# Channel attention and gated convolution: low halves last in each product, one softmax step on GpSimd, the first k loads on a second queue, native rows dealt anew

## The chip, the cores and the metric

The kernel runs on one core of a Trainium2 chip. The metric is device time in microseconds (us) of one launch, lower is better; the number that is compared is the median of several runs. A core has five engines, each with an instruction stream of its own that it works off strictly in order: TensorE (PE in the profile; its weight loads are listed apart as PEld), VectorE (DVE), ScalarE (ACT), GpSimd (POOL) and SyncE (SP, which here only issues DMAs). They meet through semaphores. TensorE writes only to PSUM, and GpSimd has no access to it.

## The reference

Four batches of q, k and v (6336 rows, 256 channels, fp32). First attention over channels, then a gated causal convolution on its result:

```python
qn = q / (np.linalg.norm(q, axis=1, keepdims=True) + 1e-06)
kn = k / (np.linalg.norm(k, axis=1, keepdims=True) + 1e-06)
s = kn.transpose(0, 2, 1) @ qn / tau          # 256 x 256 per batch
a = softmax(s)                                # over the last axis
x = v @ a
gate_pre[t] = sum over k=0..4 of conv_w[k] * x[t - 4 + k]    # zeros ahead of row 0
gate = 1 / (1 + exp(-gate_pre))
out = (gate * (x @ w_val)) @ w_out
```

## The kernel before, in words

**Split operands.** TensorE is fed fp32r, a format that it takes in one pass but which holds fewer bits than fp32. So most operands are split in two: a high half (ScalarE casts to fp32r) and a low half (what is left: GpSimd subtracts the high half from the value). A product is then the sum of three matmuls: high by high, high by low and low by high. A "native" row is not split: q and k go to TensorE as fp32, one matmul where the split takes three, at another speed; it needs the load alone, neither the cast nor the subtraction.

**Tasks and their names.** For each batch:

- `P`, rows of s: q and k come in 17 groups of up to three 128-row slices (`raw`, 384 KB each for q and k; the first group has one slice and 64 rows that are left over). Line 407 casts (`hi<-raw` on ACT), line 410 subtracts (`hi<-raw,hi` on POOL), line 475 adds both 128-channel halves to `s_ps`. `nw` (lines 376 to 379) says how many slices of a group are native. Line 434 squares q and k, and the squares are summed slice by slice on DVE into `acc_ps` or on POOL into `acc` (line 438).
- `M`, the softmax: norms, root, scaling, exponentials, division (`a`, line 556), the high and low half of `a` (`w`, lines 560 and 563), its transpose times w_val (line 579), and the high and low half of that (lines 583 and 586). So `x @ w_val` is computed as v times (a w_val).

For each of 13 steps of up to 508 rows in a batch (52 in all):

- v comes in (four DMAs), DVE transposes it (645), ACT casts (`v_hi`, 649), POOL subtracts (`v_lo`, 652).
- `X`, line 660: v times a, 12 matmuls of 512 columns into two `x_ps` banks. ACT and DVE make the gate from them: line 684 the first tap, line 687 the other four, line 698 the sigmoid. In the last stretch of the program POOL adds one tap (695).
- `U`, line 660 too: v times a w_val, into `val_ps`; DVE multiplies it with the gate (705), ACT casts (`g_hi`, 711), POOL subtracts (`g_lo`, 714).
- `F`, line 726: times w_out, 24 matmuls of 256 columns in two banks; ACT copies them out (736), SP stores (741).

**What sets the order.** The program is not written in the order in which it runs. Each task is given to `Plan` with its engine, a cost in us, what it depends on and which buffers it takes. `line`, at the end of the kernel, fixes only a due order for TensorE; `deadlines` works back from it when each task must be done, and `run` plays the whole program through with the costs, and always gives an engine the task that is due first among those that can start. The order that comes out is emitted, and each engine keeps it. A changed cost or dependency can therefore move tasks anywhere in the program. Buffers: six of `raw`, three of `hi` and of v's halves, two `x_ps` banks, four other PSUM banks.

**The start.** SP issues q and k of the first groups one by one (lines 390 and 392); ACT loads a function table at once (line 267); TensorE fills the time with matmuls on zeros (lines 457 and 464): seven ahead of the first row, two more after each of the two parts of the first group.

**The end.** The last step has two tiles of 120 rows. Both are multiplied into one bank, `o_ps`; ACT copies the first and stores it from its own queue, DVE copies the second and SP stores it (746 to 748).

## Time and profile before

| | |
|---|---|
| median of three runs | 612.95 us (612.79 to 615.64) |
| the profiled execution | 614.12 us, of which the span 612.3 |
| mean granted TensorE clock in it | 0.996 |
| busy: PE, PEld | 595.1 us (97%), 534.7 us (87%) |
| busy: DVE, ACT, POOL | 522.1 us (85%), 475.8 us (78%), 492.8 us (80%) |
| read from HBM, written | 79.18 MB, 25.95 MB |

PE's busy time is not its work: matmuls overlap, and a matmul of 256 columns is listed with 283 ns where the next one starts 120 ns later. So what TensorE loses is read here from waits (of PE and of PEld, with what ended them) and from when the next matmul starts. PEld's waits are somewhat longer than PE's for one and the same stop, since the listed end of the matmul ahead comes late.

### The profile page before, as it was taken

The page shows a single profiled execution, that of the slowest core. Times are in us where ns is not written, and L with a number is a line of the kernel's source. Part 1 is how long each engine was busy: PE and PEld are TensorE (multiplying, and loading weights), DVE is VectorE, ACT ScalarE, POOL GpSimd, SP SyncE. Part 2 cuts the span into 40 slices and gives each one's busy share as a digit, 9 for nine tenths or more (in the row PEclk, how much of TensorE's full clock was granted, in tenths as well). Part 3 has the DMA queues.
Part 4 walks back from the last instruction along what each step waited for, and adds up shares of the span by engine and source line. Part 5 has one row for each costly group of instructions (what it writes and reads, how often), then busy time and mean ns, then how long its engine had stood idle before and what let it go on. Part 6 is the DMA issues. An engine that isn't in the chain of part 4 may idle for free.

```text
span 612.3 us, 10517 instructions
## 1 busy us (share of the span) xinstructions
PE 595.1 (97%) x3660; PEld 534.7 (87%) x3660; DVE 522.1 (85%) x797; ACT 475.8 (78%) x584; POOL 492.8 (80%) x229
## 2 busy tenths in 40 slices
PE   8999899999999899999999999999999999999996
PEld 7987789999889799898998898898988898888885
DVE  3995999999797999989878899989878879888773
ACT  5787888788889787878689989787857776666763
POOL 2895879999969799999994899999963676676743
PEclk9998999999999999999999999999999999999999
DMA  8999957696775397977659678678646244554222
GB/s 280 389 306 297 258 137 162 161 213 146 203 186 176 93 232 181 189 180 197 166 139 208 193 160 215 141 203 194 137 121 137 68 135 102 124 137 120 69 67 87
DMA packets 154913, 105.84 MB, mean 173 GB/s; under 512 B 111083, under 2 KB 137963, under 8 KB 154859
## 3 DMA queue, kind: packets, MB, share of 16 engines
q1 hardware_dynamic: 154724, 105.04, 67.3%
q8 instruction: 29, 0.48, 0.3%
q14 instruction: 25, 0.20, 0.1%
q10 hardware_dynamic: 135, 0.12, 0.1%
HBM read 79.18 MB, written 25.95 MB: 172 GB/s over the span
## 4 chain that ended last, share of the span: by engine, by line
PE 45%; DVE 9%; ACT 6%; POOL 6%; issue 4%; DMA 1%; SPq 1%; POOLq 0%; DVEq 0%; ACTq 0%
PE o_ps L726 13%; PE x_ps L660 12%; PE val_ps L660 11%; PE s_ps L475 9%; DVE gate L687 6%; POOL v_lo L652 2%; POOL g_lo L714 2%; DMA v_raw<-in_v_dram 1%; DVE gate L705 1%; DVE acc_ps L438 1%; POOL hi L410 1%; POOL gate L695 1%; DVE v_raw L645 1%; ACT gate L698 1%; ACT g_hi L711 1%
## 5 line engine op out<-in xcount | busy, mean ns | idle before, releaser
L687 DVE SCALAR_TENSOR_TENSOR gate<-x_ps,wa,gate 128x508 f32<-128x508 f32 (+1 forms) x401 | 271.8, 719 | 42.0 <-ACT gate L684 21.1
L410 POOL TENSOR_TENSOR hi<-raw,hi 128x1536 fp32r<-128x1536 f32 (+2 forms) x61 | 179.9, 2958 | 6.5 <-ACT hi L407 2.9
L714 POOL TENSOR_TENSOR g_lo<-gate,g_hi 128x1016 fp32r<-128x1016 f32 (+2 forms) x52 | 121.1, 2329 | 47.9 <-ACT g_hi L711 47.1
L652 POOL TENSOR_TENSOR v_lo<-v_raw,v_hi 128x1024 fp32r<-128x1024 f32 (+1 forms) x52 | 124.1, 2387 | 23.1 <-ACT v_hi L649 21.8
L660 PE MATMUL x_ps<-v_hi,w 128*128 128x512 f32 (+2 forms) x416 | 135.3, 385 | 5.5 <-DVE gate L687 3.4
L660 PE MATMUL val_ps<-v_hi,w 128*128 128x508 f32 (+1 forms) x416 | 132.5, 381 | 0.0
L475 PE MATMUL s_ps<-hi 128*128 128x256 f32 (+1 forms) x906 | 121.0, 285 | 1.1 <-POOL hi L410 1.1
L438 DVE TENSOR_TENSOR acc_ps<-acc_ps,sq 128x512 f32<-128x512 f32 (+1 forms) x149 | 103.3, 693 | 17.6 <-ACT sq L434 13.8
L475 PEld LDWEIGHTS s_ps<-hi 128*128 128x128 f32 (+1 forms) x906 | 114.8, 196 | 3.8 <-POOL hi L410 2.2
L726 PE MATMUL o_ps<-wo_hi,g_lo 128*127 128x256 f32 (+1 forms) x400 | 113.2, 283 | 2.4 <-POOL g_lo L714 2.1
L726 PE MATMUL o_ps<-wo_hi,g_hi 128*127 128x256 f32 (+1 forms) x400 | 112.9, 282 | 0.0
L726 PE MATMUL o_ps<-wo_lo,g_hi 128*127 128x256 f32 (+1 forms) x400 | 112.6, 281 | 0.0
L434 ACT ACTIVATE sq<-raw 128x1536 f32<-128x1536 f32 (+2 forms) x68 | 95.6, 1409 | 9.6 <-DMA raw<-in_k_dram 6.7
L660 PEld LDWEIGHTS x_ps<-v_hi,w 128*128 128x128 f32 x416 | 77.4, 188 | 21.3 <-issue 4.6
L660 PEld LDWEIGHTS val_ps<-v_hi,w 128*128 128x128 f32 x416 | 77.1, 188 | 14.9
L711 ACT CAST g_hi<-gate 128x1016 fp32r<-128x1016 f32 (+3 forms) x54 | 52.6, 978 | 36.6 <-DVE gate L705 36.4
L660 PE MATMUL x_ps<-v_lo,w 128*128 128x512 f32 (+2 forms) x208 | 79.8, 384 | 1.0 <-POOL v_lo L652 1.0
L407 ACT CAST hi<-raw 128x1536 fp32r<-128x1536 f32 (+2 forms) x61 | 76.1, 1249 | 4.3 <-DMA raw<-in_k_dram 4.3
L660 PE MATMUL val_ps<-v_lo,w 128*128 128x508 f32 (+1 forms) x208 | 79.0, 380 | 0.0
L726 PEld LDWEIGHTS o_ps<-wo_hi,g_lo 128*127 128x127 f32 (+1 forms) x400 | 75.0, 188 | 3.6 <-POOL g_lo L714 3.6
L736 ACT COPY o_sb<-o_ps 127x512 f32<-127x512 f32 (+1 forms) x99 | 56.8, 585 | 26.3 <-PE o_ps L726 26.1
L726 PEld LDWEIGHTS o_ps<-wo_hi,g_hi 128*127 128x127 f32 (+1 forms) x400 | 74.9, 187 | 1.6
(78 smaller groups left out, 762.6 us busy)
## 6 DMA issues: line engine op xcount, KB each, us to landing
raw<-in_q_dram SPq DMA_DIRECT2D x64, 384.0 KB, 6.0
raw<-in_k_dram SPq DMA_DIRECT2D x64, 384.0 KB, 6.3
v_raw<-in_v_dram SPq DMA_DIRECT2D x192, 128.0 KB, 5.6
out_dram<-o_sb SPq DMA_DIRECT2D x48, 448.0 KB, 3.2
out_dram<-o_sb SPq DMA_DIRECT2D x48, 60.0 KB, 3.0
v_raw<-in_v_dram SPq DMA_DIRECT2D x16, 64.0 KB, 2.4
out_dram<-o_sb SPq DMA_DIRECT2D x3, 240.0 KB, 2.6
raw<-in_q_dram SPq DMA_DIRECT2D x4, 128.0 KB, 2.9
```

The costliest lines, as they stand in the source:

```text
L407: nc.scalar.copy(t["hi"][r, js, :, 0, :], t["raw"][r, js, :, :])
L410: nc.gpsimd.tensor_tensor(t["hi"][r, js, :, 1, :], t["raw"][r, js, :, :], t["hi"][r, js, :, 0, :].bitcast(F32), ALU.subtract)
L434: nc.scalar.activation(t["sq"][0:np_, ja:jb], t["raw"][0:np_, ja:jb], AF.Square)
L438: eng.tensor_tensor(st[key][0:np_], st[key][0:np_], t["sq"][0:np_, j], ALU.add)
L475: nc.tensor.matmul(st["s"][:, h, :], lhs, rhs, start=False, stop=stop and h == NH - 1 and n_ == len(ops) - 1)
L652: nc.gpsimd.tensor_tensor(t["vl"][:, :, 0:g, :], t["v"], t["vh"][:, :, 0:g, :].bitcast(F32), ALU.subtract)
L660: nc.tensor.matmul(dst, weights[b][:, which, ws, ch, hs], vs[:, ch, at + lo:at + hi_], start=n_ == 0, stop=n_ == 3 * NH - 1)
L687: nc.vector.scalar_tensor_tensor(t["gate"][:, h, 0:w], t["x", h][:, k_:k_ + w], cw[:, h, k_:k_ + 1], t["gate"][:, h, 0:w], ALU.mult, ALU.add)
L711: nc.scalar.copy(t["gh"][:, hs, 0:w], t["gate"][:, hs, 0:w])
L714: eng.tensor_tensor(t["gl"][:, hs, 0:w], t["gate"][:, hs, 0:w], t["gh"][:, hs, 0:w].bitcast(F32), ALU.subtract)
L726: nc.tensor.matmul(t["o", p][0:rows, u * C:(u + 1) * C], gs[:, h, j * rows:(j + 1) * rows], ws[:, h, :], start=n_ == 0, stop=n_ == 3 * NH - 1)
L736: nc.scalar.copy(t["o_sb"][0:rows, pair[0]:pair[0] + len(pair), :], t["o", p][0:rows, 0:len(pair) * C].rearrange("p (j c) -> p j c", c=C))
```

## The change

It has five parts, and the planner lays the whole program out again with them.

1. In X and U the matmuls that read v's low half come last within each bank, in F those that read g's low half come last over both tiles of a bank (`HEADS`), and rows of s that are split become two tasks: high by high needs the cast alone, the other two the subtraction too. The planner is told by `lead` how much later than the start of a task such an operand is needed. In the first step of each batch, the low half of the softmax's weights comes last instead.
2. The softmax's `low` (before: line 563, DVE) is a GpSimd instruction, with a cost of 1.25 instead of 0.61.
3. The k loads of the first two groups are issued by ACT, and its table load stands behind them. Three instead of six matmuls on zeros follow the first one, and none follows the first slice.
4. Native rows: in batch 0 all slices of groups 0 to 2 and of the last, and two of each other (before: all of 0 to 4); in batch 1 two slices of groups 0 to 4 (before: three of 0 to 3). That is 47 instead of 49.
5. The last step's two tiles go to two banks (`x_ps`), each copied when its own matmuls are done; the store of the step ahead of it is issued in two parts.

```diff
-SIDE = 5
+SIDE = 3
...
-            nw = GROUP if g < SIDE else 2
+            nw = GROUP if g < SIDE or g == NG - 1 else 2
         else:
-            nw = GROUP if b == 1 and g < LEAD else 0
+            nw = 2 if b == 1 and g <= LEAD else 0
...
+                eng = nc.scalar if b == 0 and g < 2 and s else nc.sync
...
+            if (b, g) == (0, 1):
+                tc.keep_in_program_order(nc.scalar.activation(dummy, ones[:, 0:1], AF.Sqrt))
...
             if b == 0:
-                idle(6)
+                idle(3)
...
-            if (b, g) == (0, 0):
+            if (b, g) == (0, 0) and j == n:
                 idle(2)
...
+        for name, side, halves in (("hi", "C", ((0, 0),)), ("lo", "O", ((0, 1), (1, 0)))):
+            for u, (np_, ja, jb) in enumerate(split):
+                for j in range(ja, jb):
+                    task(("P", b, g, j, name), "PE", 0.24 * len(halves), lambda np_=np_, j=j, halves=halves: mms(np_, j, False, halves),
+                         deps=[(side, b, g, u), ("clear", b)], uses=[hi_i, ("s_ps", b)])
...
         def low():
-            nc.vector.tensor_tensor(weights[b][:, 0, 1], t["a"], weights[b][:, 0, 0].bitcast(F32), ALU.subtract)
+            nc.gpsimd.tensor_tensor(weights[b][:, 0, 1], t["a"], weights[b][:, 0, 0].bitcast(F32), ALU.subtract)
...
-            for ch in range(NH):
-                for ws, vs in ((0, th), (0, tl), (1, th)):
...
+            ops = [(ws, vs, ch) for ws, vs in ((0, th), (0, tl), (1, th))[::1 if new and not which else -1] for ch in range(NH)]
+            ops.sort(key=lambda x: (x[0], x[1] is tl) != (0, False))
...
+            ops = [(gs, ws, h) for gs, ws in ((t["gh"], wo_hi), (t["gh"], wo_lo), (t["gl"], wo_hi)) for h in range(NH)]
+            if HEADS:
+                order = [(u, n_) for n_s in (range(2 * NH), range(2 * NH, 3 * NH)) for u in range(len(pairs[p])) for n_ in n_s]
...
+                 lead={("W", n): first_lo if new else last_lo, ("M", b, "low"): last_lo if new else 0} if h == 0 else {})
...
+                 uses=[g_i, o_ps_i], takes=[o_ps_i], lead={x: (0.47 * len(pairs[p]) if HEADS else 0.47) for x in low_done} if p == 0 else {})
```

What this does to the order on the engines, at three places. First TensorE at the end of batch 0's rows and the start of its softmax (`s_ps<-raw`: native rows, two matmuls for a slice; `s_ps<-hi`: split ones, six for a slice; `ones,acc_all`: the norms). Before:

```order
L475 MATMUL s_ps<-hi 128x256 x6
L475 MATMUL s_ps<-raw 128x256 x4
L475 MATMUL s_ps<-hi 128x256 x6
L502 MATMUL o_ps<-ones,acc_all 128x1 x4
L457 MATMUL s_ps<-zeros 128x512
L475 MATMUL s_ps<-raw 128x256 x4
L534 MATMUL o_ps<-diag,ones 128x128 x2
```

With the change:

```order
L481 MATMUL s_ps<-hi 128x256 x6
L481 MATMUL s_ps<-raw 128x256 x6
L514 MATMUL o_ps<-ones,acc_all 128x1 x4
L463 MATMUL s_ps<-zeros 128x512
L481 MATMUL s_ps<-raw 128x256 x4
L546 MATMUL o_ps<-diag,ones 128x128 x2
```

Three native slices now stand between the last split slice and the norms.

Second, TensorE a little later, where the first X of the program waits for the softmax's weights (`ident,a`: the transposes, `wa,at`: the product with w_val). Before:

```order
L475 MATMUL s_ps<-raw 128x256 x18
L569 MATMUL o_ps<-ident,a 128x128 x4
L660 MATMUL x_ps<-v_hi,w 128x508
L660 MATMUL x_ps<-v_lo,w 128x508
L660 MATMUL x_ps<-v_hi,w 128x508 x2
L660 MATMUL x_ps<-v_lo,w 128x508
L660 MATMUL x_ps<-v_hi,w 128x508
L579 MATMUL o_ps<-wa,at 128x256 x4
```

With the change:

```order
L481 MATMUL s_ps<-raw 128x256 x4
L481 MATMUL s_ps<-hi 128x256 x2
L581 MATMUL o_ps<-ident,a 128x128 x4
L481 MATMUL s_ps<-hi 128x256 x4
L591 MATMUL o_ps<-wa,at 128x256 x4
L674 MATMUL x_ps<-v_hi,w 128x508 x2
L674 MATMUL x_ps<-v_lo,w 128x508 x2
L674 MATMUL x_ps<-v_hi,w 128x508 x4
L674 MATMUL x_ps<-v_lo,w 128x508 x2
L674 MATMUL x_ps<-v_hi,w 128x508 x2
```

The product with w_val and rests of rows stand ahead of X, and within X the third that needs the low half of the weights comes last.

Third, GpSimd at the second softmax. Before:

```order
L714 TENSOR_TENSOR g_lo<-gate,g_hi 128x1016
L652 TENSOR_TENSOR v_lo<-v_raw,v_hi 128x2x256
L714 TENSOR_TENSOR g_lo<-gate,g_hi 128x1016
L410 TENSOR_TENSOR hi<-raw,hi 128x6x256 x3
L652 TENSOR_TENSOR v_lo<-v_raw,v_hi 128x1024
```

With the change:

```order
L727 TENSOR_TENSOR g_lo<-gate,g_hi 128x1016
L666 TENSOR_TENSOR v_lo<-v_raw,v_hi 128x2x256
L416 TENSOR_TENSOR hi<-raw,hi 128x6x256
L575 TENSOR_TENSOR w<-a,w 128x512
L416 TENSOR_TENSOR hi<-raw,hi 128x6x256
L727 TENSOR_TENSOR g_lo<-gate,g_hi 128x1016
L666 TENSOR_TENSOR v_lo<-v_raw,v_hi 128x1024
```

`w<-a,w` is the step that was on VectorE. Over the whole program GpSimd is given 4 of these, 19 instead of 14 subtractions for one slice and 44 instead of 45 for three, and 47 instead of 43 additions of squares; VectorE loses the 4 and 4 additions; TensorE has 94 instead of 98 native matmuls of 128 rows, 918 instead of 906 split ones and 9 instead of 14 on zeros.

More of the change, by code (lines that the diff above doesn't have):

```diff
@@ L51, in deadlines @@
             clock += self.tasks[key]["cost"]
-        after = {key: set() for key in self.tasks}
+        after = {key: {} for key in self.tasks}
         for key, t in self.tasks.items():
             for d in t["deps"]:
-                after[d].add(key)
+                after[d][key] = t["lead"].get(d, 0.0)
         self.users, made = {}, {}
@@ L79, in deadlines @@
             own = self.duration(t)
-            late = min((done[x] for x in after[key]), default=clock) - own - HOP - (FLIGHT if isinstance(t["cost"], tuple) else 0)
+            late = min((done[x] + lead for x, lead in after[key].items()), default=clock) - own - HOP - (FLIGHT if isinstance(t["cost"], tuple) else 0)
             if key[0] in "YR":
                 late = min(late, due["F", key[1], key[2] if key[0] == "Y" else 0] + (4 if key[0] == "Y" else 8))
+            if key[0] == "Q":
+                late -= FLIGHT
             late = min(late, WANTED.get(key, clock))
@@ L173, in run @@
             for x in after[key]:
-                at[x] = max(at[x], end)
+                at[x] = max(at[x], end - T[x]["lead"].get(key, 0.0))
                 missing[x] -= 1
@@ L477, in mms @@
                 idle(2)
         if g == 0:
-            task(("clear", b), "PE", 3.0 if b == 0 else 0.3, clear, uses=[("s_ps", b)], takes=[("s_ps", b)])
+            task(("clear", b), "PE", 1.7 if b == 0 else 0.3, clear, uses=[("s_ps", b)], takes=[("s_ps", b)])
             rows_of[b, g].append(("clear", b))
         for np_, j in rows:
-            u = [x for x, (sn, ja, jb) in enumerate(split) if sn == np_ and ja <= j < jb]
-            task(("P", b, g, j), "PE", (0.72 if u else 0.864) + (0.9 if (b, g) == (0, 0) else 0), lambda np_=np_, j=j: mms(np_, j),
-                 deps=[("O", b, g, u[0]) if u else ("L", b, g), ("clear", b)], uses=[raw_i, ("s_ps", b)] + ([hi_i] if u else []))
@@ L604, in softmax_tasks @@
         task(k_("high"), "ACT", 0.52, high, deps=[k_("divide")])
-        task(k_("low"), "DVE", 0.61, low, deps=[k_("high")])
+        task(k_("low"), "POOL", 1.25, low, deps=[k_("high")])
         task(k_("transpose"), "PE", 0.45, transpose, deps=[k_("divide")], uses=[at_i], takes=[at_i])
@@ L635, in step_tasks @@
         end = n == NS - 1
+        new = i == 0
+        first_lo, last_lo = 0.45 * part, 0.9 * part
         def load():
@@ L737, in out_copy, with store @@
                            t["o", p][0:rows, 0:len(pair) * C].rearrange("p (j c) -> p j c", c=C))
[L739 removed]
+        def store(a, z):
             for r0, r1 in even(rows):
[L741 removed]
+                nc.sync.dma_start(out=dst[r0:r1, a:z, :], in_=t["o_sb"][r0:r1, a:z, :])
         def out_end(u):
@@ L745, in out_end @@
             o_end = raw_p.tile([P, C], F32, name="o_end", tag="raw")
-            copy(o_end[0:rows], t["o", 0][0:rows, u * C:(u + 1) * C])
+            copy(o_end[0:rows], t["o", u][0:rows, 0:C])
             for r0, r1 in even(rows):
@@ L773, in step_tasks @@
             val_i = ("bank", n, "val", h)
-            task(("U", n, h), "PE", 1.38 * part, lambda h=h: value(h), deps=[("W", n), ("M", b, "low_w")], uses=[vs_i, val_i], takes=[val_i])
+            task(("U", n, h), "PE", 1.38 * part, lambda h=h: value(h), deps=[("W", n), ("M", b, "low_w")], uses=[vs_i, val_i], takes=[val_i],
+                 lead={("M", b, "low_w"): last_lo if new and h == 0 else 0})
             task(("B", n, h), "DVE", 0.06 + 0.54 * part, lambda h=h: times(h), deps=[("U", n, h), ("Z", n)], uses=[val_i, gate_i])
```

75 lines of the change are left out of this document (41 added, 34 removed).

## The prediction, made before the changed kernel was run

> **What bounds the kernel now.** I read the shares and the chain of waits first, then the windows, then PE's and PEld's waits.
>
> ```profile
> span 612.3 us, 10517 instructions
> PE 45%; DVE 9%; ACT 6%; POOL 6%; issue 4%; DMA 1%; SPq 1%; POOLq 0%; DVEq 0%; ACTq 0%
> 209.50 2.16 PE s_ps L475 x18
> core 0: us, PE busy (x) PEld busy (x) DVE busy (x) ACT busy (x) POOL busy (x), PEclk, DMA share, GB/s
> 90.00:165.00 75.00, 75.00 (x484) 68.45 (x484) 70.19 (x104) 61.91 (x69) 73.03 (x30) 1.00 0.77 178
> 165.00:210.00 45.00, 41.79 (x274) 37.70 (x273) 39.05 (x63) 38.53 (x53) 36.49 (x16) 1.00 0.54 151
> ```
>
> Where the chain says PE, matmuls stand back to back (18 of 256 columns in 2.16 us, 0.12 each). From 90 to 165 us PE is never idle and POOL hardly (73.0 of 75). There nothing is to be won. PE loses time only at the start, around the softmaxes (165 to 210: 3.2 us idle) and near the end. What it waits for:
>
> ```profile
> PEld x_ps L660 <- issue: 4.6, 7, 1.5
> PEld o_ps L726 <- POOL g_lo L714: 3.6, 6, 1.3
> PEld x_ps L660 <- DVE w L563: 2.3, 1, 2.3
> PEld s_ps L475 <- POOL hi L410: 2.2, 4, 1.5
> PEld x_ps L660 <- POOL v_lo L652: 1.4, 1, 1.4
> PE x_ps L660 <- DVE gate L687: 3.4, 5, 1.3
> PE o_ps L726 <- POOL g_lo L714: 2.1, 3, 1.1
> PE x_ps L660 <- DVE w L563: 1.9, 1, 1.9
> ```
>
> The first row of PEld and the DVE gate row of PE are the same stops: X waits until DVE has read an `x_ps` bank. So 14.1 us of waits within the run, plus the clock and the start below, are all that can come back; TensorE's work itself hardly changes.
>
> **Part by part.** I cost it against the profiled execution.
>
> *(a) Start.*
>
> ```profile
> 0.74 1.28 ACT L267 ACT_TABLE_LOAD   x1 [0.74 <-PEq L873]
> 1.81 0.58 SPq L390 DMA_DIRECT2D raw<-in_k_dram  x1
> 2.19 2.77 PE L464 MATMUL s_ps<-zeros 128*128 128x512 f32 x6
> 4.28 0.60 ACT L429 ACTIVATE acc_ps<-raw 128x512 f32<-128x512 f32 x1 [2.05 <-DMA raw<-in_k_dram]
> 4.75 1.91 PE L475 MATMUL s_ps<-raw 128*128 128x256 f32 x4
> 6.09 1.19 PE L464 MATMUL s_ps<-zeros 128*128 128x512 f32 x2
> 7.21 1.14 PE L475 MATMUL s_ps<-raw 64*128 64x256 f32 x4
> 8.85 12.25 PE L475 MATMUL s_ps<-raw 128*128 128x256 f32 x56
> ```
>
> ACT is free at 0.74, so k of the first group goes out 1.07 earlier than SP's 1.81, and the first slice can start at 3.7; four matmuls on zeros instead of seven are done by then (2.19 plus three of 0.46). The two matmuls on zeros between 6.09 and 7.21 fall away: 1.12 more. At best the second group starts 2.2 earlier than 8.85. But the first slice takes 1.91 for four listed matmuls, where 56 take 12.25 (0.22 each, 0.875 a slice): PE is still at half clock there. If the clock rises when it did, both parts of the first group run slowly, twice 1.7 from 3.7 on, and two matmuls on zeros follow: 7.5. I take −1.3; ends −2.2 and −0.5 (the clock rises later by a stretch like the slow one in (b), 3.4 us at half speed, +1.7). SP's queue gets shorter by three issues, so later groups come no later. ACT's table load moves behind three issues of about 0.5 and ends at 3.8, before the 4.28 of ACT's first work; without that cover the first squares would come some 0.5 late, and no matmul of the first groups waits for them.
>
> The Trainium skill (TensorE: Matmul & The Clock Gate, Part 1) says that the clock is granted per free-running window of about 3.4 us and falls to half after an idle one; by it the fewer matmuls on zeros can leave PE cold for one window more, which is the upper end above and a rival below.
>
> *(b) End of batch 0.*
>
> ```profile
> 46.47 1.89 PE L475 MATMUL s_ps<-raw 128*128 128x256 f32 x8
> 49.47 0.99 PE L475 MATMUL s_ps<-hi 128*128 128x256 f32 x6 [1.11 <-POOL hi L410]
> 51.62 3.56 PE L475 MATMUL s_ps<-raw 128*128 128x256 f32 x8
> 47.50:51.20 3.70, 2.59 (x19) 2.16 (x18) 2.19 (x3) 1.79 (x3) 1.91 (x2) 1.00 0.96 354
> 51.20:54.70 3.50, 3.50 (x9) 2.40 (x9) 0.74 (x4) 3.38 (x6) 2.04 (x1) 0.51 1.00 384
> ```
>
> PE waits 1.1 us (PEld 1.5) for the last split slice. Behind this idle stretch PEclk is 0.51: eight matmuls take 3.56 instead of 1.89. With the change three native slices (2.6 us) stand behind that slice, so its wait goes, −1.3 (ends −1.5 and 0), and with it the cause of the half clock, −1.7 (ends −1.7 and 0, since the 128x1 norms also leave PE little to do there). What is late next is the square sum; it has the same 2.6 us.
>
> *(c) Native rows.* A native slice costs 0.875, a split one 0.72 (six of 0.12): two fewer, −0.3. Five more casts on ACT, at 78%, hide.
>
> *(d) First X.*
>
> ```profile
> 62.33 3.47 POOL L410 TENSOR_TENSOR hi<-raw,hi 128x1536 fp32r<-128x1536 f32 x1 [0.83 <-ACT hi L407]
> 62.80 3.55 DVE L563 TENSOR_TENSOR w<-a,w 128x512 fp32r<-128x512 f32 x1
> L563 DVE TENSOR_TENSOR w<-a,w x4: 650/3230/3552, 62.8 to 479.7; 128x512 fp32r<-128x512 f32 x4
> L438 POOL TENSOR_TENSOR acc<-acc,sq 128x512 f32<-128x512 f32 x42 | 54.6, 1301 | 15.9 <-ACT sq L434 14.0 <-ACT acc L429 1.2
> ```
>
> The subtraction takes 0.65 at its fastest and 3.55 here; it ends just after POOL's subtraction, in whose shadow it stood. On POOL I price it as the addition of the same shape, 1.30 (it may be 0.65, as on DVE, or 3.5, if it is held up in turn; nearest is the addition). X now has the product with w_val ahead of it (eight listed matmuls like the native ones, 1.75) and four of its six matmuls (0.9) before the low half. That covers 1.30 and a late start of more than 1 us. −1.9 (ends −2.3 and 0).
>
> *(e) Second softmax.*
>
> ```profile
> 186.95 7.01 POOL L410 TENSOR_TENSOR hi<-raw,hi 128x1536 fp32r<-128x1536 f32 x2
> 191.09 3.42 DVE L563 TENSOR_TENSOR w<-a,w 128x512 fp32r<-128x512 f32 x1 [3.08 <-ACT w L560]
> PEld x_ps L660 <- issue: 2.6, 2, 1.5
> ```
>
> DVE idles 3.08 for the cast and then works 3.42, until POOL is done; the taps behind it come late, and X at 200 to 203 waits 2.6 (PE's own rows: 2.2) for them. Both leave DVE, so −2.0 (ends −2.6 and 0). The wait for the cast goes to POOL, where subtractions for s and g are queued behind it; they are due some microseconds later.
>
> *(f) F.* The low half was read by the third matmul, 0.24 after the start; now by the ninth, 0.95. Each of six stops shrinks by 0.71: all but the one of 1.3 vanish. 3.6 less 0.6: −2.9 (ends −3.6 and 0).
>
> *(g) v's low half.* One stop of 1.4, cover 0.23 before and 0.92 now: −0.7 (ends −1.4 and 0).
>
> *(h) Tail.*
>
> ```profile
> 607.14 0.42 DVE L746 COPY o_end<-o_ps 120x256 f32<-120x256 f32 x1 [1.21 <-PE o_ps L726]
> 607.60 0.37 ACT L746 COPY o_end<-o_ps 120x256 f32<-120x256 f32 x1 [1.31 <-DVE o_end L746]
> 608.00 0.63 ACTq L748 DMA_DIRECT2D out_dram<-o_end  x1
> ```
>
> ACT's copy waits for DVE's of the same bank. With two banks ACT's is done earlier and DVE's is the last: its store goes out 0.4 earlier. −0.4 (ends −0.9 and 0). Two more store issues hide under F.
>
> *(i) The new order.* It will have stops of its own, since the planner spends the new cover where it can. Ends: 0, and 7.2 (all of g_lo, hi and v_lo again). I take 2.2, about a third.
>
> Sum: −1.3 −3.0 −0.3 −1.9 −2.0 −2.9 −0.7 −0.4 +2.2 = −10.3. The profiled execution took 614.12, 1.2 more than the median; from the median 612.95 this gives 602.7, said as 603.
>
> **Rivals.**
>
> *The cover is spent.* The planner starts F and X as much earlier as `lead` allows; then its errors meet PE as before. (f) and (g) are lost and half of (d): 603 + 3.6 + 0.9 = 607.5. For it: those stops come from a plan that also meant to have none. Against: in most of them the engines' order leaves PE nothing to start earlier with.
>
> *The front is fed too slowly.*
>
> ```profile
> 82.94 0.47 PE L660 MATMUL x_ps<-v_hi,w 128*128 128x512 f32 x1 [0.27 <-DVE gate L687]
> 63.00:83.00 20.00, 17.81 (x106) 15.53 (x104) 18.31 (x22) 17.48 (x18) 16.11 (x6) 1.00 1.18 260
> ```
>
> Up to the third step's X at 82.94 the DMA engines are full (share above 1) and DVE works 18.3 of 20 us; in batch 0 a group needs two POOL instructions of 1.3, against PE's 2.47 for two native slices and a split one. If one of these sets the pace up to there, (a), (b) and (d) come back as other waits: 603 + 1.3 + 3.0 + 1.9 = 609.2. Against: DVE is relieved of 2.9 us there, and POOL idles 3.9 of these 20.
>
> *GpSimd becomes the bound (slower).* The order gives it 4 subtractions w (5.2), five more of one slice and one less of three (3.0), four additions (5.2): 13.4 us more on 492.8. Where it has 2 us left in 75 it would hold PE up. It decides once what is added in such a stretch exceeds that rest; if all of it did, 603 + 13.4 = 616. Against: the w stand at the softmaxes, where POOL idles 8.5 of 45, and the planner can give additions back to DVE.
>
> *A longer cold start.* With fewer matmuls on zeros the clock could stay at half for one more stretch as long as that in (b): 3.4 us at half speed, +1.7, so 604.7. For it: PE has less to do ahead of 3.7 than before. Against: it is then busy without a gap. Beside it stands the rule of the Trainium skill named in (a); the trace agrees with its length of a stretch, but when it falls in another execution no run here shows.
>
> **How the numbers follow.** Forecast 0.55, cover spent 0.18, slow front 0.12, longer cold start 0.07, GpSimd 0.08. The range reaches from the case that the new order costs nothing and (a) and (f) come in full (603 − 2.2 − 0.9 − 0.7 = 599, and a little for (e)) up to the slow front: 598.5 to 609.8. Half a percent is about what a measurement of this kernel can tell from no change; it ends at 609.9. All cases but the last are under it, the slow front only just, so I give a third of that and part of the others' spread to no change: faster 0.84, same 0.09, slower 0.07.
>
> **What would show it.** The second group's native matmuls start near 7.5; no PEclk near 0.5 between 45 and 60 us; `w` on POOL near 1.3, and no DVE subtraction of 3 us; X of the third step starts about 7 us earlier than at 82.94; PEld's wait for g_lo under 1 us; the last store issued 0.4 after DVE's last copy starts. I am wrong if PEld's waits for POOL in sum are not smaller than the 7.2 of before, or if waits for DMA take the place of those for w and hi ahead of 83 us.

## The result, and the profile after

The changed kernel took 606.36 us (median; 604.14 to 606.84), the kernel before 613.15 beside it. The ratio is 0.9873, with a 95% interval of 0.9852 to 0.9894: 1.3% faster. The forecast was 603.0 in a range of 598.5 to 609.8. The profiled execution took 606.84 with a span of 605.0, which is 7.3 less than before, where the sum of the forecast was 10.3.

From the page of the changed kernel, the busy shares:

```profile
PE 594.2 (98%) x3659; PEld 533.2 (88%) x3659; DVE 510.2 (84%) x789; ACT 474.3 (78%) x588; POOL 504.1 (83%) x241
```

PEld's waits (us in total, times, longest):

```profile
PEld o_ps L746 <- POOL g_lo L727: 2.7, 4, 1.1
PEld s_ps L481 <- POOL hi L416: 2.7, 4, 1.0
PEld x_ps L674 <- issue: 2.3, 4, 0.9
PEld s_ps L481 <- DMA raw<-in_q_dram: 1.0, 2, 0.7
PEld s_ps L481 <- DMA raw<-in_k_dram: 0.8, 1, 0.8
```

And the group of softmax's subtraction, now on POOL (sum, mean ns):

```profile
L575 POOL TENSOR_TENSOR w<-a,w 128x512 fp32r<-128x512 f32 x4 | 5.2, 1310 | 0.0
```

It takes 1.31, as priced. The wait of 2.3 for `w` is gone, X's waits for its bank are halved (4.6 to 2.3), those for `g_lo` have only gone from 3.6 to 2.7, those for `hi` have grown from 2.2 to 2.7, and there are new ones for transfers, 1.8. PEld's waits for POOL sum to 5.4, against 7.2 before.

Where the time came from is read stage by stage. The next two views cut both runs at the same five products: the third step's X, the eleventh step's X behind the second batch's norms, the start of the eleventh step's F behind the second softmax, the last but one step's X, and the end. Columns: stretch, its length, then busy time (and instructions) of PE, PEld, DVE, ACT and POOL, then PEclk. Before:

```profile
0.00:82.94 82.94, 78.06 (x394) 67.98 (x395) 62.45 (x104) 62.40 (x72) 57.90 (x43) 0.98 1.02 306
82.94:173.43 90.49, 89.84 (x572) 81.44 (x573) 84.52 (x125) 74.34 (x84) 87.36 (x36) 1.00 0.67 156
173.43:206.49 33.06, 30.35 (x188) 26.79 (x186) 28.27 (x44) 29.46 (x41) 24.55 (x11) 1.00 0.69 188
206.49:585.44 378.95, 376.66 (x2373) 340.28 (x2371) 333.49 (x502) 297.43 (x370) 313.12 (x137) 1.00 0.63 152
585.44:612.30 26.86, 20.22 (x139) 18.24 (x137) 13.39 (x26) 12.17 (x21) 9.90 (x6) 0.98 0.30 88
```

and after:

```profile
0.00:80.78 80.78, 77.39 (x394) 66.21 (x395) 60.72 (x103) 62.32 (x75) 61.69 (x49) 1.00 1.06 313
80.78:169.94 89.16, 89.16 (x575) 81.29 (x574) 85.27 (x125) 75.91 (x85) 88.12 (x37) 1.00 0.67 160
169.94:200.04 30.10, 30.10 (x188) 26.89 (x186) 22.25 (x38) 28.09 (x39) 24.57 (x11) 1.00 0.66 175
200.04:577.24 377.20, 375.49 (x2366) 339.12 (x2365) 325.13 (x496) 295.01 (x369) 318.23 (x140) 1.00 0.66 156
577.24:605.00 27.76, 22.02 (x146) 19.69 (x144) 16.80 (x31) 13.02 (x22) 11.53 (x8) 0.99 0.28 85
```

The lengths differ by −2.16, −1.33, −2.96, −1.75 and +0.90, in sum −7.3. The second softmax gave most and runs without any idle time of PE now (30.10 of 30.10, before 30.35 of 33.06). The front, for which the forecast had 6.5 (steps a to d), gave 2.2, and all of it in its second half: at the product with which the softmax scales its norms, behind the same work on PE but for one slice dealt natively or split, the two kernels stand level (before, after):

```profile
55.10 0.71 PE L534 MATMUL o_ps<-diag,ones 128*128 128x128 f32 x4
55.06 0.71 PE L546 MATMUL o_ps<-diag,ones 128*128 128x128 f32 x4
```

The last stretch holds 1.8 more of PE's work, since half a U more lies in it; its idle time went from 6.6 to 5.7.

What became of the gain of its first half shows in the start. PE's first native slices, after:

```profile
3.70 4.08 PE L481 MATMUL s_ps<-raw 128*128 128x256 f32 x8
8.72 3.63 PE L481 MATMUL s_ps<-raw 128*128 128x256 f32 x12
```

The first slice starts at 3.70 as forecast, but the second group only at 8.72 (8.85 before), and its first four matmuls run at half pace, 0.43 each, where all took 0.22 before. Over the twelve of the row that is 0.30 in the mean; the twelfth starts at 11.98, 0.8 later than before.

### The profile page after: what moved, and what is told of

Its sections match the earlier page's. It is cut to its first block, busy times and chain, and to the rows that moved or that the text cites. A ratio compares the mean times of both kernels' runs of the same rounds, so it can differ in the third digit from the quotient of the medians.

```text
span 605.0 us, 10549 instructions
## 1 busy us (share of the span) xinstructions
PE 594.2 (98%) x3659; PEld 533.2 (88%) x3659; DVE 510.2 (84%) x789; ACT 474.3 (78%) x588; POOL 504.1 (83%) x241
## 4 chain that ended last, share of the span: by engine, by line
PE 52%; DVE 24%; POOL 7%; issue 6%; ACT 6%; DMA 4%; SPq 1%; POOLq 0%; DVEq 0%; ACTq 0%
PE s_ps L481 13%; PE x_ps L674 13%; DVE gate L700 12%; PE o_ps L746 12%; PE val_ps L674 12%; DVE acc_ps L444 6%; POOL g_lo L727 3%; DVE gate L718 3%; DMA v_raw<-in_v_dram 2%; DMA raw<-in_k_dram 2%; POOL gate L708 1%; DVE v_raw L659 1%; POOL hi L416 1%; ACT g_hi L724 1%; PE o_ps L591 1%
## 5 line engine op out<-in xcount | busy, mean ns | idle before, releaser
L481 PE MATMUL s_ps<-hi 128*128 128x256 f32 x918 | 126.5, 288 | 1.3 <-POOL hi L416 1.3
L481 PEld LDWEIGHTS s_ps<-hi 128*128 128x128 f32 x918 | 117.9, 196 | 4.8 <-POOL hi L416 2.7
L674 PE MATMUL x_ps<-v_hi,w 128*128 128x512 f32 (+2 forms) x416 | 110.3, 385 | 1.5 <-DVE gate L700 1.5
L746 PE MATMUL o_ps<-wo_hi,g_hi 128*127 128x256 f32 (+1 forms) x396 | 79.2, 281 | 0.0
L746 PE MATMUL o_ps<-wo_lo,g_hi 128*127 128x256 f32 (+1 forms) x396 | 79.0, 281 | 0.0
L444 POOL TENSOR_TENSOR acc<-acc,sq 128x512 f32<-128x512 f32 (+1 forms) x47 | 61.1, 1301 | 14.4 <-ACT sq L440 12.7
L718 DVE TENSOR_TENSOR gate<-val_ps,gate 128x508 f32<-128x508 f32 (+1 forms) x104 | 67.0, 656 | 4.3 <-ACT gate L711 4.3
L697 ACT ACTIVATE gate<-x_ps,wa 128x508 f32<-128x508 f32 (+1 forms) x104 | 68.2, 662 | 1.2 <-PE x_ps L674 1.1
L711 ACT ACTIVATE gate<-gate 128x1016 f32<-128x1016 f32 (+1 forms) x52 | 53.2, 1024 | 18.5 <-DVE gate L700 18.5
L746 PE MATMUL o_ps<-wo_hi,g_lo 128*127 128x256 f32 (+1 forms) x396 | 64.0, 284 | 1.9 <-POOL g_lo L727 1.9
```

The lines of the kernel that those rows point to most:

```text
L444: eng.tensor_tensor(st[key][0:np_], st[key][0:np_], t["sq"][0:np_, j], ALU.add)
L481: nc.tensor.matmul(st["s"][:, h, :], lhs, rhs, start=False, stop=stop and h == NH - 1 and n_ == len(ops) - 1)
L674: nc.tensor.matmul(dst, weights[b][:, which, ws, ch, hs], vs[:, ch, at + lo:at + hi_], start=n_ == 0, stop=n_ == len(ops) - 1)
L697: nc.scalar.activation(t["gate"][:, h, 0:w], t["x", h][:, 0:w], AF.Copy, scale=cw[:, h, 0:1])
L718: nc.vector.tensor_tensor(t["gate"][:, h, 0:w], t["val", h][:, 0:w], t["gate"][:, h, 0:w], ALU.mult)
L746: nc.tensor.matmul(t["o", p][0:rows, u * C:(u + 1) * C], gs[:, h, j * rows:(j + 1) * rows], ws[:, h, :], start=(u, n_) == (0, 0) if HEADS ...
```

## The experiments

All ratios are to the kernel before, run on the same chip. The change itself stands at 0.9873 [0.9852, 0.9894]. An uncertainty given with a difference is half the width of its 95% interval, worked out from the two intervals. "Order kept" means that the planner made the order of the tasks for the unedited kernel; "planned anew" that it made it for the edited one.

**The start undone, order kept.**

```diff
-                eng = nc.scalar if b == 0 and g < 2 and s else nc.sync
+                eng = nc.sync
-                idle(3)
+                idle(6)
-            if (b, g) == (0, 0) and j == n:
+            if (b, g) == (0, 0):
```

with the Sqrt table load first on ScalarE again.

> The change with its start undone: both k loads of the first two groups issued by SP again, the Sqrt table load first on ScalarE, seven matmuls on zeros ahead of the first slice and two behind each of its parts; the order of everything else is the one of the change. Theory A (the forecast's step a): the new start is worth 1.3 us, so this is 1.3 slower than the change, about 607.7 (ratio to before 0.989). Theory B (read from the trace of the change: the second group starts at 8.72 instead of 8.85, but eight of its matmuls run at 0.43 instead of 0.22): the new start costs 1.6 and this is 1 to 1.6 faster, about 605 (ratio 0.985); the second group's matmuls take 0.22 each from the first on, and k and q of the second group have landed by about 7.5 instead of 8.5.

Measured: 0.9886 [0.9855, 0.9917]. The second group starts at 8.57 and is at full pace from its first matmul, as theory B says. Its price was too high: in the change four matmuls ran at 0.43, not eight, and the start cost 0.8, not 1.6. The time isn't below the change's: in the profiled execution PE stops 3.1 us for a split slice at 38 us, behind an operation that this edit doesn't touch (the next run explains it). The interval holds both theories.

**Only the second group's k back on SP, order kept.**

```diff
-                eng = nc.scalar if b == 0 and g < 2 and s else nc.sync
+                eng = nc.scalar if b == 0 and g < 1 and s else nc.sync
```

> The change with only the first group's k issued by ScalarE and the second group's k by SP. If the second group comes late because two queues share the engines (its q landed at 8.50 and k at 8.32, against 6.50 and 7.41 before), both land by 7.7 here and its matmuls start at about 7.8 to 8.0 instead of 8.72; the time falls by up to 0.9 if the clock rises at the same moment after the first work or earlier, and by nothing if the clock rises at about 10.3 again, since all work ahead of it then runs at half pace. If the queue has nothing to do with it, the landings stay at 8.3 to 8.5.

Measured: 0.9842 [0.9816, 0.9869], median 604.86. The transfers of 384 KB issued from 1.5 to 3.65 us and their time to landing (a median where there are two); before, after, and in this run:

```profile
raw<-in_q_dram SPq DMA_DIRECT2D x1, 384.0 KB, 3.6
raw<-in_k_dram SPq DMA_DIRECT2D x1, 384.0 KB, 3.8
```

```profile
raw<-in_q_dram SPq DMA_DIRECT2D x2, 384.0 KB, 6.7
raw<-in_k_dram ACTq DMA_DIRECT2D x1, 384.0 KB, 6.6
```

```profile
raw<-in_q_dram SPq DMA_DIRECT2D x2, 384.0 KB, 4.6
raw<-in_k_dram SPq DMA_DIRECT2D x2, 384.0 KB, 5.2
```

PE in this run:

```profile
3.77 3.06 PE L481 MATMUL s_ps<-raw 128*128 128x256 f32 x8
7.34 4.92 PE L481 MATMUL s_ps<-raw 128*128 128x256 f32 x22
```

With k and q of the second group issued side by side from two queues, each takes 6.6 to 6.7 to land, and both come in later than from one queue, though issued earlier. That is what the Trainium skill says (DMA: Bandwidth & Descriptors, "Issuing engines are not separate DMA queues"): transfers of different engines run on the same 16 DMA engines and interleave; the trace agrees. Here the second group starts at 7.34, the 7.5 that the forecast had, and all its matmuls are at full pace (22 in 4.92). By the ratios this is 1.9 below the change, with an uncertainty of 2.1. How much of it the queue brings isn't shown: PE came to full pace at 5.6 us here and at 10.5 in the change, and a later run with this start came to it at 13.2.

The profiled execution of this kernel took 607.99, 3.1 above its median. Its trace shows why, in the same stretch in which the run before stopped. Left to right: start, duration; in brackets idle time ahead and its releaser:

```profile
27.03 4.47 DVE L329 TENSOR_SCALAR w_raw<-w_raw 128x512 int32<-128x512 int32 x1
32.94 1.49 ACT L440 ACTIVATE sq<-raw 128x1536 f32<-128x1536 f32 x1 [3.74 <-DVE acc_ps L444]
34.56 1.28 POOL L444 TENSOR_TENSOR acc<-acc,sq 128x512 f32<-128x512 f32 x1 [3.35 <-ACT sq L440]
37.13 1.65 PE L481 MATMUL s_ps<-hi 128*128 128x256 f32 x6 [3.14 <-POOL hi L416]
```

One integer operation of the weights' preparation takes 4.47 on DVE; the squares wait for DVE's addition behind it, POOL waits for the squares, and PE for POOL, 3.1 us. The trace's records of the granted clock then show half from 36.27 us on, for 6.83 us; beside the change, PE lost 2.8 by the stop and 2.7 more up to 40 us at half pace, and made up 1.6 of it by 48 us. In the changed kernel the same operation took 3.19:

```profile
27.74 3.19 DVE L329 TENSOR_SCALAR w_raw<-w_raw 128x512 int32<-128x512 int32 x1
```

There the squares waited 1.93 behind it. It is the same stall that the forecast saw for DVE's subtraction `w`, at an operation that the forecast did not look at.

**That operation into PSUM, in the run above.**

```diff
-            nc.vector.tensor_scalar(up, up, 0xFFE00, 3, ALU.bitwise_and, ALU.logical_shift_left)
+            m = ps.tile([P, 512], F32, name="x_ps", bufs=2)[:, 0:n].bitcast(I32)
+            nc.vector.tensor_scalar(m, up, 0xFFE00, 3, ALU.bitwise_and, ALU.logical_shift_left)
...
-            nc.vector.tensor_tensor(up, up, f, ALU.bitwise_or)
+            nc.vector.tensor_tensor(up, up, m, ALU.bitwise_or)
```

(the sign is set into `up` between the two).

> The change with the second group's k on SP (as in the run e9_k1_on_sp), and with one integer operation of the weights' preparation writing to a PSUM bank instead of to SBUF: TENSOR_SCALAR w_raw<-w_raw took 0.42 us when GpSimd was idle, but 3.19 in the change and 4.47 in e9_k1_on_sp, ending with GpSimd's run of subtractions, and behind it the squares, and with them the matmuls, waited 3.1 us. Theory C: DVE was held up because this operation has all its operands in SBUF beside GpSimd's; from PSUM it takes 0.7 in any case, the wait of 3.1 at 37 us disappears and the time is 2 to 3.5 below e9_k1_on_sp (602 to 603, ratio 0.979 to 0.981). Rival: the transfers bound this stretch in any case and less than 1 us comes back. Rival: the slow one was the operation's place in the order, not its operands: the same 3 to 4.5 us in PSUM.

Measured: 0.9840 [0.9817, 0.9863], median 604.61, profiled execution 603.42. The operation's group (count, sum, mean ns):

```profile
L333 DVE TENSOR_SCALAR x_ps<-w_raw 128x512 int32<-128x512 int32 x2 | 1.4, 684 | 0.0
```

The stretch from 26 to 40 us, first in the run above and then in this one:

```profile
26.00:40.00 14.00, 10.86 (x56) 9.52 (x55) 13.83 (x17) 7.45 (x8) 10.20 (x9) 0.87 1.03 396
```

```profile
26.00:40.00 14.00, 14.00 (x81) 12.49 (x81) 13.70 (x22) 10.42 (x11) 12.45 (x11) 1.00 1.03 399
```

0.68 each time, and PE is busy for 14.00 of 14, not 10.86. POOL was at work both times: the first, from 26.63 to 27.32, lies wholly inside one of its additions (26.52 to 27.81). So theory C holds for the mechanism: the same step at the same place no longer stalls when its result goes to PSUM. The Trainium skill (SBUF — State Buffer, "SBUF: two separate sides") calls this an exclusive lock: an operation of DVE that uses the shared pair of ports, and GpSimd, block each other for the whole instruction. The traces agree that the operation stands while POOL works, but not on how long: it takes 0.42 at its fastest in the change, and where it takes 3.19, 4.44 or 4.47 it starts beside one addition of POOL (1.3 us) and ends only behind the next two or three of POOL's instructions. In the run without leads (below), at the same place beside the same addition, it was done in 0.77. The price of theory C did not come. For the median nothing is gained (604.61 against 604.86), as its first rival has it: the profiled execution of the run above lost 3.1 against its own median, which fits an operation that is not caught in every execution. That is inferred; the other executions have no trace.

**Softmax's low half on VectorE again, order kept.**

```diff
-            nc.gpsimd.tensor_tensor(weights[b][:, 0, 1], t["a"], ...
+            nc.vector.tensor_tensor(weights[b][:, 0, 1], t["a"], ...
```

> The change with softmax's low half w computed by VectorE again, at the place in the order where GpSimd had it. Theory A (steps d and e): up to 1.9 + 2.0 = 3.9 slower than the change (about 610), with a subtraction of 3 us or more on DVE at one softmax or another. Rival: the new order of the matmuls in X covers the low half in any case, and where it is computed is worth nothing: within 1 us of the change.

**The same, planned anew** (the task also declared as 0.61 on VectorE).

> The change with softmax's low half w on VectorE, and the planner told so (0.61 on VectorE instead of 1.25 on GpSimd), so that it makes an order for it. The run with the old order kept (e2_w_low_dve) was 6.8 us slower than the change. Theory A (steps d and e as sized): 1.9 + 2.0 = 3.9 slower than the change. Theory B: 6.8 came in part from an order made for GpSimd; the price of w on VectorE in an order made for it is what the kernel before gained from the move alone (0.4 measured, 1.7 in the spans of the profiled executions) with that of the order of X (2.2 measured): 1 to 3 slower. Theory C: VectorE's blocked subtractions (3.5 at three softmaxes) cost what they cost in any order: 6 or more slower.

Measured: 0.9984 [0.9964, 1.0004] with the order kept, 0.9884 [0.9847, 0.9921] planned anew. The first loses 6.8 us to the change, more than steps d and e together, the second 0.7, with an uncertainty of 2.6. The group of `w` in the two:

```profile
L575 DVE TENSOR_TENSOR w<-a,w 128x512 fp32r<-128x512 f32 x4 | 8.5, 2132 | 0.0
```

```profile
L575 DVE TENSOR_TENSOR w<-a,w 128x512 fp32r<-128x512 f32 x4 | 5.0, 1248 | 5.9 <-ACT w L572 5.9
```

With the order kept, two of the four stand beside a POOL subtraction of 3.5 and take 3.52 and 3.57. The second softmax, between the same X and F as above, then takes 34.52 instead of 30.10, 2.6 of it idle time of PE and 1.7 a stretch at half clock behind that; the third loses some 3:

```profile
169.92:204.44 34.52, 31.93 (x187) 28.34 (x186) 26.86 (x41) 29.09 (x41) 24.04 (x11) 0.95 0.72 178
```

Where the planner knows that `w` stands on DVE, none of the four is beside such a long subtraction; they take 1.16 to 1.43, and the second softmax runs as fast as in the change (30.10 us from the same X to the same F, with PE busy throughout). So GpSimd is not needed to avoid the stall; another order avoids it too. Theories A (3.9) and C (6 or more) are out as sized; B's 1 to 3 and no loss at all both lie in the interval.

**Only `w` on GpSimd, in the kernel before, order kept**; and **the same with the low halves last in X and U**.

```diff
-            nc.vector.tensor_tensor(weights[b][:, 0, 1], t["a"], ...
+            nc.gpsimd.tensor_tensor(weights[b][:, 0, 1], t["a"], ...
```

> The kernel before with one part of the change: softmax's low half w computed by GpSimd at the place where VectorE did it, everything else as before. Theory A (steps d and e): the subtraction takes 1.3 on GpSimd; the taps of the second softmax come some 2 earlier (-2.0 to -2.6), while at the first softmax the subtraction waits behind the 3.47 one and ends 0.7 later than before; sum -1.3 to -2, ratio about 0.997. Theory B (read from the run with w on VectorE in the change, which lost 4.4 at the second softmax and 3 at the third): the third softmax gains too, -3 to -4. Rival: GpSimd's own queue is what bounds there, and nothing is gained.

> As the run before it, and X and U take their products in the change's order too (low halves last). Theory A (steps d, e, g): 1 to 2 more than the run before it is gained, since four of X's six matmuls now stand ahead of the low half at the first softmax (0.9) and ahead of v's low half at the last step (0.7). Rival: the order of the products is worth nothing once w is on GpSimd.

Measured: 0.9993 [0.9973, 1.0014] and 0.9964 [0.9940, 0.9989]. From the first, the stretch around the second softmax (before: 33.06 long, PE busy 30.35), and behind it waits of PEld:

```profile
173.47:204.50 31.03, 30.12 (x188) 26.72 (x187) 24.76 (x43) 29.29 (x41) 25.55 (x12) 1.00 0.75 200
```

```profile
PEld x_ps L660 <- POOL w L563: 3.1, 1, 3.1
PEld o_ps L726 <- POOL g_lo L714: 4.2, 6, 1.6
```

Step e comes out as sized: the stretch is 2.0 shorter, and X's waits for its bank in it go from 2.6 to 0.8. Theory B's gain at the third softmax isn't there. But at the first softmax `w` now waits in POOL's queue and X waits 3.1 for it instead of 2.3, and F's waits for `g_lo` grow from 3.6 to 4.2, because POOL has more to do. The span fell by 1.7 (612.3 to 610.6), but 1.0 of that stands already at the scaling of the norms, ahead of the first `w`: the kernel before had a stretch at half clock there, and this execution had none. Behind it the move brings 0.7, and 0.4 by the ratio. With the low halves last, the waits for `w` and for v's low half shrink to 2.7 and 0.7; that version is 2.2 us faster than the kernel before (0.7 to 3.7 by the interval). Against the run without them it is 1.8, with an uncertainty of 2.0: theory A's 1 to 2 fits, and the rival, nothing, isn't excluded.

**Only F's order, in the kernel before, order of tasks kept**; and **F's old order in the change, order of tasks kept** (`HEADS = False` and the old list of products; the leads stay). The first edit:

```diff
-                for h in range(NH):
-                    for gs, ws in ((t["gh"], wo_hi), (t["gh"], wo_lo), (t["gl"], wo_hi)):
+            ops = [(gs, ws, h) for gs, ws in ((t["gh"], wo_hi), (t["gh"], wo_lo), (t["gl"], wo_hi)) for h in range(NH)]
```

> The kernel before with one part of the change: F's products in the new order (the low half of g read by the ninth matmul and later), the order of all tasks as before. Theory A (step f): the six stops for g_lo shrink by 0.71 each and 2.8 to 2.9 us come back (ratio about 0.9953), with PEld's wait for g_lo under 1 us. Theory B: time won at one of these stops is given back at the next one that does not depend on it (a softmax, a transfer): 1 to 1.5 come back. Rival: nothing, the low half being late everywhere by as much as it is read later.

> The change with F's products taken in the old order (the low half of g read by the third matmul, not by the ninth), the order of the tasks as the change has it. Theory A (step f, the forecast): 2.9 or a little more slower than the change (about 609.5). Theory B (the new order spent the cover: stops for g_lo in the change still sum to 2.4 to 2.7): each of its three or four stops grows by 0.71 and a few F that are now just in time stop too, 2 to 6 slower. Rival: F's stops are set by what comes behind them, and the time changes by less than 1.

Measured: 0.9993 [0.9977, 1.0010] and 0.9878 [0.9849, 0.9907]. PEld's waits for `g_lo`, of the first and of the second:

```profile
PEld o_ps L727 <- POOL g_lo L714: 1.8, 3, 0.9
PEld x_ps L660 <- POOL v_lo L652: 2.0, 2, 1.8
```

```profile
PEld o_ps L746 <- POOL g_lo L727: 5.4, 10, 1.3
```

The order of the matmuls does what it says: in the kernel before it halves the waits (3.6 to 1.8) and undoing it in the change doubles them (2.7 to 5.4). What that is worth in time is not settled. In the kernel before it is 0.4 by the ratio, at most 1.4 by the interval, and 1.0 by the spans of one execution each; the wait for v's low half in the last but one step grew from 1.4 to 1.8 meanwhile. Theory A's 2.9 is out; theory B's 1 to 1.5 and the rival, nothing, both fit. In the change the old order costs 0.3 by the ratio, with an uncertainty of 2.2, as the rival says; but in the two profiled executions X of the third step starts 0.3 later with it and X of the last but one step 3.0 later, so 2.7 are lost between them, as much as the waits grew.

**The native rows dealt as before, planned anew.**

```diff
-SIDE = 3
+SIDE = 5
-            nw = GROUP if g < SIDE or g == NG - 1 else 2
+            nw = GROUP if g < SIDE else 2
-            nw = 2 if b == 1 and g <= LEAD else 0
+            nw = GROUP if b == 1 and g < LEAD else 0
```

> The change with the 47 native rows dealt as before (the first five groups of the first batch wholly native, its last group split; the first four groups of the second batch wholly native), planned anew. Theory A (steps b and c): the wait of 1.3 for the last split slice at 48 us, a stretch of PEclk near 0.5 behind it (1.7) and 0.3 of work come back: up to 3.3 slower than the change. Theory B (from the trace of the change: native slices at the end of the batch, but stops of 0.49, 0.76 and 0.57 for the split slices of the groups ahead of it, which the transfers and GpSimd feed too slowly): the gain and the new stops cancel, within 1 us of the change, or a little faster.

Measured: 0.9869 [0.9831, 0.9907]: the change without its new deal is as fast (0.2 less, with an uncertainty of 2.7), and theory A's 3.3 is out. Between 45 and 60 us neither the wait for the last split slice nor a stretch at half clock returned: PE goes into that slice at 49.20 without a stop. So the new deal is not what removes this wait; another order of the tasks does it too. And the half clock is no sure follower of the stop: four kernels have it, of 1.10 to 1.11 us (the kernel before and those with only `w` moved, with X and U besides, and with only F's order), and it came behind it in two of them. The kernel before and the one with only `w` moved, from 51.2 to 54.7 us:

```profile
51.20:54.70 3.50, 3.50 (x9) 2.40 (x9) 0.74 (x4) 3.38 (x6) 2.04 (x1) 0.51 1.00 384
```

```profile
51.20:54.70 3.50, 3.50 (x21) 2.73 (x21) 0.74 (x4) 3.27 (x6) 1.39 (x1) 1.00 0.94 322
```

**The planner not told of the late reading.**

```diff
-        self.tasks[key] = dict(..., lead=dict(lead), uses=...
+        self.tasks[key] = dict(..., lead={}, uses=...
```

> The change with the planner not told that the low half is read late (all leads zero), the matmuls' order as in the change, planned anew. Rival of the forecast (the cover is spent): with the leads the planner starts F and X as much earlier as the cover allows; without them they are planned for when the low half is there, and the stops for g_lo (2.7 in PEld's waits) fall under 1: 1 to 2 faster than the change. Theory A: the cover is mostly not spent, since in most stops PE has nothing else to start: PEld's wait for g_lo stays within 0.7 of 2.7, and the time within 1. Third way: a stop that the planner expects makes it put other work ahead of F, and what waits for F's buffers then comes late: slower.

Measured: 0.9859 [0.9819, 0.9899], median 605.09. PEld has no wait for `g_lo` left. So the 2.7 that the change still had were made by the plan, as the rival "the cover is spent" says. But others came in their place, at X (2.9 for its bank, 1.1 for v's low half) and in the softmaxes (1.2 for `diag`), and the time is no different within the interval (0.9 lower, with an uncertainty of 2.8). The rival named the right cause for the stops that stayed, and too high a price.

**The three edits that stood lowest, together** (no leads, second group's k on SP, the integer operation into PSUM).

> The three edits together that each stood below the change: no leads (order of the run e4_no_lead), the second group's k on SP, and the integer operation of the weights' preparation into PSUM. In e4_no_lead that operation took 0.77 and was not held up, so it can bring nothing here beyond keeping it so; the start brings the second group's matmuls from 8.79 to about 7.4. If the front up to 50 us keeps this gain: 1.3 below e4_no_lead (ratio 0.9838 or a little less, span of the profiled execution about 601.5). If the transfers bound the front anyway, the gain is gone by the norms at 49 us and the time is that of e4_no_lead (0.986).

Measured: 0.9837 [0.9818, 0.9856], median 605.34. The three versions with the second group's k on SP stand at 0.9842, 0.9840 and 0.9837, some 2 us below the change; the intervals still touch. Against the run without leads the ratio is 1.3 lower, as expected, but the intervals overlap and the medians are level. The start of this kernel is the one of the run with k on SP, instruction for instruction on PE, and yet (PE's rows, and then a stretch):

```profile
3.80 4.08 PE L487 MATMUL s_ps<-raw 128*128 128x256 f32 x8
8.83 3.61 PE L487 MATMUL s_ps<-raw 128*128 128x256 f32 x8
```

```profile
8.80:12.30 3.50, 3.50 (x10) 2.75 (x9) 1.80 (x3) 2.21 (x3) 2.29 (x2) 1.00 1.01 391
```

Eight matmuls took 4.08 here and 3.06 there. From 8.8 to 12.3 us PE, busy throughout, got 10 done here; the same stretch there:

```profile
8.80:12.30 3.50, 3.50 (x18) 3.18 (x17) 1.75 (x3) 2.18 (x3) 2.24 (x2) 1.00 1.03 402
```

## Why the prediction was right, and where it was not

The time lies in the range and the sign is right; the sum of 10.3 was 3 too high. The stages above, by the profiled executions, against the steps that fall in them:

| | forecast | measured |
|---|---|---|
| up to the scaling of the norms, 55 us: (a), (b), (c) | −4.6 | 0.0 |
| from there to the third step's X: (d) | −1.9 | −2.1 |
| the second softmax: (e) | −2.0 | −3.0 |
| all else: (f) to (i) | −1.8 | −2.2 |

(A part of (c) falls behind 55 us.) So the forecast failed at the start and at the end of batch 0; that the rest comes near is in part luck, since the single steps behind the last line, and the way in which (d) was won, came out otherwise. By its steps:

- *(a) Start*, −1.3. Failed in two places. It took an earlier issue for an earlier landing: the second group's k left 1.8 earlier and both halves landed later (6.6 and 6.7 to land, against 3.6 and 3.8). And the clock rose later, which was the rival "a longer cold start", at about the price that the rival named: by the trace's records full clock begins at 10.5 us, at 6.9 before, and 3.6 us at half pace are 1.8. The start cost 0.8 in the profiled execution.
- *(b) End of batch 0*, −3.0. The half clock is gone in this execution (1.00 from 51.2 to 54.7), −1.7. The wait of 1.1 came back in pieces for the groups ahead:

```profile
36.58 0.99 PE L481 MATMUL s_ps<-hi 128*128 128x256 f32 x6 [0.33 <-POOL hi L416]
44.83 0.99 PE L481 MATMUL s_ps<-hi 128*128 128x256 f32 x6 [0.60 <-POOL hi L416]
47.96 0.99 PE L481 MATMUL s_ps<-hi 128*128 128x256 f32 x6 [0.40 <-POOL hi L416]
51.78 1.08 PE L514 MATMUL o_ps<-ones,acc_all 128*128 128x1 f32 x8 [0.24 <-DVE acc_all L518]
```

  That is the rival "the front is fed too slowly" in part: 1.6 of idle time, with the norms at 51.78 instead of 50.29. What fed too slowly was not what the rival named (full DMA engines, a busy DVE) alone, but also, it seems, DVE caught by POOL for 3.19: in the version without leads, where the same operation took 0.77, the norms start at 49.34. The term also took the clock drop for a property of the kernel, though it came in two of four executions with the same stop; and the old deal, planned anew, has neither the stop nor the drop.
- *(c) Native rows*, −0.3: too small to be seen; the whole deal undone changes nothing measurable.
- *(d) First X*, −1.9. As forecast, and by the first of the two covers that the step names: `w` is done at 64.74, while PE works on the product with w_val, before X starts; the second cover, X's own four matmuls, wasn't needed. What the step didn't have is that POOL comes to `w` straight behind a v subtraction, not behind one of 3.47:

```profile
63.46 1.28 POOL L575 TENSOR_TENSOR w<-a,w 128x512 fp32r<-128x512 f32 x1
63.75 1.99 PE L591 MATMUL o_ps<-wa,at 128*128 128x256 f32 x8 [0.20 <-ACT at L585]
65.39 0.81 PE L674 MATMUL x_ps<-v_hi,w 128*128 128x508 f32 x2
```

  With the old order of tasks GpSimd alone made the wait longer (3.1). X itself starts 1.6 later than before (65.39 against 63.79), since that product, which stood behind half of it, now stands ahead.
- *(e) Second softmax*, −2.0: measured −2.0 by the move alone, −2.96 in the change.
- *(f) F*, −2.9: mis-sized for the kernel before, where it halves the waits and brings 1.0 by the spans, 1.4 at most by the interval; the step counted each shortened stop as time won. In the change the traces put 2.7 on it and the medians 0.3; that stays open.
- *(g) v's low half*, −0.7: 1.4 to 0.7 with X's order and `w` moved, as worked out; in the change PE has no wait for it at all.
- *(h) Tail*, −0.4. DVE's copy starts at 601.03 and the last store is issued at 601.48, as forecast. From the last store's issue to the end of the span it is 3.5 now and 4.3 before, which the step did not have.
- *(i) New stops*, +2.2: what the trace shows of new waits (1.8 for transfers, 0.5 more for `hi`, with 2.7 for `g_lo` left where 0.6 were forecast) is of that size or more, and the gaps of (a) and (b) come on top.

Of the signs that the prediction named, three failed: the second group starts at 8.72, not near 7.5; the third step's X comes 2.2 earlier, not 7; the waits for `g_lo` are 2.7, not under 1. Of its two signs of being wrong the first is not met (waits for POOL 5.4 against 7.2), the second is: ahead of 83 us the waits for `hi` and for transfers are 2.7 and 1.8, together the 4.5 that `w` and `hi` took before. That is the failure of (a) and (b) once more.

"GpSimd becomes the bound" did not happen: POOL is busy for 504.1 of 605.0, 11.3 more than before, near the 13.4 that were counted.

What carries the gain is settled only in part. At the second softmax the cause is shown from both sides: `w` moved to GpSimd in the kernel before takes 2.0 from it, `w` moved back in the change adds 4.4. For the other 4.3 it isn't. No edit put into the kernel before brought more than 0.4%. Undoing one in the change took back nothing beyond the interval (the start and F's order with the order of tasks kept; the native deal, `w` and the leads with a new plan); only `w` on DVE in an order made for GpSimd did. With uncertainties of 2 us and more, a part worth 1 to 2 us would not have shown in them. The parts are not terms of a sum: each gives the planner another order, and an order avoids stops that a part was made for. What all versions near 606 have in common and no run tried alone is the split of a slice's products into a task that needs only the cast and one that needs POOL's half, together with the low-last order of X and U and the tail. Whether that split is what lets the planner avoid the stops stays open.

## What to carry to other kernels

Where a planner sets the order, cost a change stage by stage and expect stops that it removes to come back as others until a stage shows no idle time at all; undo one part with the order kept and again with a new plan, since the two can differ by the whole gain (6.8 us against 0.7). Look for operations of DVE whose shortest and longest execution differ several times over: beside a busy GpSimd they are the stalls, and a result in PSUM instead of SBUF took one of them away. Don't issue transfers that are needed together from two queues in the hope that they land sooner.

## What the runs showed of the hardware that was not expected

- The granted clock in the profile's rows does not show the cold start: from 8.8 to 12.3 us the row reads 1.00 with 10 matmuls done, and 1.00 with 18. The traces hold no record of the clock ahead of its rise (at 13.2 us in the first, 5.6 in the second), and the row counts that time as full. The pace has to be read from the matmuls' own times.
- With seven matmuls on zeros ahead of the first slice and two behind it, the second part of the first group, from 6.9 to 7.3 us on, ran at full pace in each of the five kernels that start so; with four and none, the pace rose between 5.6 and 13.6 us in nine kernels, also among kernels with the same instructions on PE. The Trainium skill (TensorE: Matmul & The Clock Gate, Part 1) says that the clock rises after at least one busy window of about 3.4 us, that the warm-up takes about that time, and that the windows run freely. The traces agree on the windows: in each of the seven with a drop, every change of the clock lies a whole number of 3.41 us after its rise (in the kernel before it falls 13 of them later, and comes back after one more). That PE was still at half pace at 12.3 us in the last run above, busy for 8.5 of the 8.6 us from 3.7 on, does not agree with a warm-up of one window. What the matmuls on zeros have that the native ones lack isn't settled.
- A clock drop came behind a stop of PE of only 1.1 us, for 3.41 us in one execution and for 6.83 in another, and not in two more with the same stop.
- An integer TENSOR_SCALAR of 128x512 on DVE took 0.42 to 0.77 us where POOL held it up little or not, 1.33 to 1.47 where it started beside one of POOL's instructions and ended just behind it, 3.19 to 4.47 where it ended two or three further on, and 0.68 to 0.69 with the result in PSUM.
